# Score and maxima matmuls over 64 rows instead of 50 and 48, with zero rows behind

## The chip, the cores and the metric

One core of a Trainium2 chip runs the kernel. The time is device microseconds of one execution; the median of the runs is compared. TensorE is called PE in the profile (PEld is its loading of weights), VectorE DVE, ScalarE ACT, GpSimd POOL and SyncE, which issues most DMAs, SP.

## The reference

```python
x = A_x                                              # 1 x 2048 x 512
g = sigmoid((x * gate_w).sum(-1, keepdims=True))
a = dft_seq_re @ (x @ dft_hid_re.T) - dft_seq_im @ (x @ dft_hid_im.T)
q, k, v = split(x @ wqkv)                            # 32 heads of 16
b = concat(softmax(q @ k.T / 4) @ v) @ wo            # full attention, 2048 x 2048 per head
out = g * a + (1 - g) * b
```

All is float32.

## The kernel before

The sequence is 2048 long (16 tiles of 128, NT), the width 512 (4 tiles, KT). Products that need accuracy are done with numbers split into a high and a low part (`hi_lo`, L100), so that each takes three matmuls.

The stages, in order of time: q and k for all heads are computed and their high and low parts stored to DRAM (`evac_qk`, L200, through seven `hl` buffers on chip); then V (first eight tiles over all 128 rows, L397, then pairs of tiles on the two halves of the array, L365), its tiles emptied from PSUM by a copy on ScalarE and one on VectorE (`v_done`, L338 and L339); then x times the imaginary hidden DFT (L365 too). From there on the attention runs beside the other products of the reference.

Attention works on pairs of heads (16 pairs). For one pair `load_stacks` (L263) brings q and k from DRAM into `qs` and `ks`, tiles of 128 partitions by 2048, of which there are two each, used by turns. Each head has one half of the partitions, 64 rows from row 0 or 64: the first 48 hold three times 16 rows of high and low parts, so that one matmul over 48 rows gives the three products q_hi k_hi + q_hi k_lo + q_lo k_hi. The *maxima* matmul (`a_tile`, L278, matmul in L284) uses these 48 rows; VectorE reduces each result of 128 x 512 to the row's maxima (L286). When half of a pair's rows is done, `m_parts` and `m_rows` (L293 to L310) turn the negated maxima, high and low, into rows and write them by DMA into rows 48 and 49 of `qs` (L309, on SP or GpSimd). Rows 48 and 49 of `ks` hold ones; they are written once for each of the two tiles, by eight DMAs at the start (L322 to L325). The *score* matmul (`scores`, L761, matmul in L774) runs over 50 rows, and so yields scores with the maximum taken off; ScalarE takes their exponential (L775), and `pv` (L788, matmuls in L796) multiplies by V.

The order of the work on TensorE is written out by hand. In each segment (`segment`, L907) one half of the array does products of the DFT (64 rows, L451) while the other half does scores ("s") and maxima ("a"), and then both do `pv` ("|"). The digits name PSUM banks; scores and maxima use six:

```python
FULL = "s2 a3 s4 a1 s5 s2 a0 s3 a4 s1 a5 s2 a0 s3 a4 a1 | |"
```

FULL segments fill the long middle stage. Maxima run ahead of scores by LEAD = 44 steps of 64 per pair; the first 44 are done during the V and DFT products (`phase`, L358). V tiles use the three banks of `psS`. A plan by units (32 per pair) says when other work is issued; `load_stacks(p)` for p from 1 comes at unit 32 (p - 1) (L854, L855). SP issues its DMAs, and VectorE, ScalarE and GpSimd take their instructions, in the order in which the program writes them.

The tiles `vt`, `qs` and `ks` lie where the buffers of the q/k stage were. The lines around L317 set up what attention needs: ones on GpSimd, the ones of `vt`, `load_stacks(0)`, four loads of `wo`, the eight DMAs into `ks`.

Of the kernel before, what the change touches and what calls it, by code (L numbers as in the profile page):

```python
# [9 lines left out]
F32 = mybir.dt.float32  # L10
# [6 lines left out]
S = 2048  # L17
# [14 lines left out]
def mix_kernel(ctx: ExitStack, tc: tile.TileContext, xa_t, xa, wqkv, w_hid, w_seq, wo, gate_w, out):  # L32
# [5 lines left out]
    nc = tc.nc  # L38
# [31 lines left out]
    dram = ctx.enter_context(tc.tile_pool(name="dram", bufs=1, space=DRAM))  # L70
# [7 lines left out]
    yr_d = [dram.tile([P, D], F32, name=f"yr{t}") for t in range(NT)]  # L78
    yg_d = [dram.tile([P, D], F32, name=f"yg{t}") for t in range(NT)]

    wo_d = [dram.tile([P, 2, D], F32, name=f"wo{kt}") for kt in range(KT)]
    oh_d = [[dram.tile([P, 2, S // 2], F32, name=f"oh{hf}{ct}") for ct in range(3)] for hf in range(2)]
    r_d = [[dram.tile([2, 4, S // 2], F32, name=f"r{hf}{ct}") for ct in range(4)] for hf in range(2)]
# [4 lines left out]
    z = const.tile([P, NT], F32, name="z")  # L88
# [31 lines left out]
    def staged(src):  # L120
        raw = st1.tile([P, D], F32, name="raw", bufs=RAW)
        i = nc.sync.dma_start(raw, src)
        if behind:
            tc.add_manual_dep(i.ins, behind.pop().ins.name,
                              mybir.DependencyInfo(mybir.DependencyClass.Sync, mybir.DependencyReason.DATA))
        return raw
# [64 lines left out]
    with tc.tile_pool(name="qk", bufs=1, reuse_waits="tile") as pool:  # L191
# [38 lines left out]
        for tb in range(4):  # L230
# [4 lines left out]
            for c in range(2):  # L235
                if tb == 0 and c == 0:
                    pss = [bank() for _ in range(4)]
                    for kt in range(KT):
                        x = xab[tb][:, :, :, kt * P:(kt + 1) * P]
# [20 lines left out]
    qs = [main.tile([P, S], F32R, name=f"qs{i}", tag=f"qs{i}") for i in range(2)]  # L260
    ks = [main.tile([P, S], F32R, name=f"ks{i}", tag=f"ks{i}") for i in range(2)]

    def load_stacks(p):  # L263
        q_t, k_t = qs[p % 2], ks[p % 2]
        for h in range(2):
            rows = slice((2 * p + h) * DH, (2 * p + h + 1) * DH)
            o = 64 * h

            for i, (qv, kv) in enumerate(((0, 0), (0, 1), (1, 0))):
                part = slice(o + 16 * i, o + 16 * i + 16)  # L270
                nc.sync.dma_start(q_t[part].bitcast(F32), qk_d[0][qv, rows])
                nc.sync.dma_start(k_t[part].bitcast(F32), qk_d[1][kv, rows])


    deferred = []
# [2 lines left out]
    def a_tile(i, h, ps=None, bank=None):  # L278
        p, j = divmod(i, 64)
        qt, kb = divmod(j, 4)  # L280
        if ps is None:
            ps = psA.tile([P, 512], F32, "a", bank)
        r = slice(64 * h, 64 * h + 48)
        nc.tensor.matmul(ps, qs[p % 2][r, qt * P:(qt + 1) * P], ks[p % 2][r, kb * 512:(kb + 1) * 512],  # L284
                         start=True, stop=True)
        user = nc.vector.tensor_reduce(mx[p % 2][:, h, qt, kb:kb + 1], ps, AX.X, ALU.max)  # L286
        hf = j // 32
        a_left[p, hf] = a_left.get((p, hf), 64) - 1
        if not a_left[p, hf]:
            deferred.extend((partial(m_parts, p, hf), partial(m_rows, p, hf)))  # L290
        return user
# [22 lines left out]
            deferred.pop(0)()  # L314


    ones = st1.tile([2, 2 * D], F32, name="hl", bufs=4)  # L317
    nc.gpsimd.memset(ones, 1.0)
    nc.gpsimd.memset(vt[:, :, :, 16:17], 1.0)
    load_stacks(0)  # L320
    wos = [staged(wo[:, kt]) for kt in range(KT)]
    for i in range(2):  # L322
        for h in range(2):
# [34 lines left out]
    def phase(pair, half, maxima):  # L358
        nonlocal a_next, user
        before, user = user, None  # L360
        for j in range(12):
            for x, (ps, ops, done) in enumerate(pair):
                st, mv = ops[j]
                r = slice(64 * (half ^ x), 64 * (half ^ x) + 64)
                i = nc.tensor.matmul(ps, st[r], mv[r], start=not half and not j, stop=half == 1 and j == 11)  # L365
                if not j and not x and half:
                    tc.add_manual_dep(i.ins, before.ins.name,
                                      mybir.DependencyInfo(mybir.DependencyClass.Sync, mybir.DependencyReason.DATA))
            if maxima and j in (3, 9):
                for h in range(2):  # L370
                    used = a_tile(a_next, h, acc if h and j == 9 else None)
                user = user or used
                a_next += 1
        if half:
            for ps, ops, done in pair:
                done(ps)
        if deferred:
            deferred.pop(0)()
# [382 lines left out]
    def scores(u, qb, h, bank=(psS, "s"), number=None):  # L761
        p, r = divmod(u, 32)
        hf, kt = divmod(r, 16)
        q0 = hf * 1024 + qb * 512
        if u >= UNITS - 16:

            blk, kt = divmod(kt, 8)
            q0, kt = 1024 + blk * 512, 2 * kt + qb
        if u not in pts:
            pts[u] = work.tile([P, 4, 512], F32, name="pt", bufs=4)  # L770
        pool, name = bank
        ps = pool.tile([P, 512], F32, name=name) if number is None else pool.tile([P, 512], F32, name, number)
        rr = slice(64 * h, 64 * h + 50)
        nc.tensor.matmul(ps, ks[p % 2][rr, kt * P:(kt + 1) * P], qs[p % 2][rr, q0:q0 + 512], start=True, stop=True)  # L774
        return nc.scalar.activation(pts[u][:, 2 * qb + h], ps, AF.Exp, bias=0.0, scale=DH ** -0.5)  # L775

# [77 lines left out]
    for p in range(1, NP):  # L854
        at(32 * (p - 1), load_stacks, p)  # L855
# [37 lines left out]
    def score(kind, h, number=None):  # L893
        nonlocal exponential
        x = next(streams[h][kind == "a"], None)
        if x:
            users.append((kind, a_tile(*x, bank=number) if kind == "a" else scores(*x, number=number)))
            if kind == "s":
                exponential = users[-1][1]
# [84 lines left out]
    for bank in (*three[:1], *three):  # L984
        scores(*next(streams[1][0]), bank)
# [8 lines left out]
    for u in range(valued + 2, UNITS, 2):  # L994
        run_plan(u)
        for i in range(4):
            if i == 2:
                for gen, n in whole[u]:
                    pump(gen, n)
                if u == 506:  # L1000
                    last_pairs[0].turn()
                elif u == 508:
                    last_pairs[0].back()
            for h in range(2):
                scores(u + i // 2, i % 2, h, three[h])
        values()
        values()
# [40 lines left out]
```

## Time and profile before

| what | value |
|---|---|
| median of 3 runs | 1698.75 us (1698.6 to 1699.33) |
| span of the profiled execution | 1696.8 us |
| PE busy | 1689.2 us |
| DVE busy | 1366.7 us |
| ACT busy | 1138.6 us |
| POOL busy | 449.6 us |
| mean granted TensorE clock | 0.999 |

The span goes from the first to the last instruction of one profiled execution; the time of a run holds a little more than that. Rows of groups read: line, engine, operation, what it writes and from what, shapes, count | busy time, mean ns of one | idle time of the engine before them and what ended it. Rows in order of time read: start in us, duration in us, engine, line, operation, count and, in brackets, idle time before. "SPq" is the queue of SyncE. Names drop buffer numbers: `hl` is a pair of high and low parts, `acc` the result of `pv`, `pt` the exponentials, `mx` the maxima, `d` a PSUM bank of the DFT products.

### The profile page before, as it was taken

The page shows a single profiled execution, that of the slowest core. Times are in us where ns is not written, and L with a number is a line of the kernel's source. Part 1 is how long each engine was busy: PE and PEld are TensorE (multiplying, and loading weights), DVE is VectorE, ACT ScalarE, POOL GpSimd, SP SyncE. Part 2 cuts the span into 40 slices and gives each one's busy share as a digit, 9 for nine tenths or more (in the row PEclk, how much of TensorE's full clock was granted, in tenths as well). Part 3 has the DMA queues.
Part 4 walks back from the last instruction along what each step waited for, and adds up shares of the span by engine and source line. Part 5 has one row for each costly group of instructions (what it writes and reads, how often), then busy time and mean ns, then how long its engine had stood idle before and what let it go on. Part 6 is the DMA issues. An engine that isn't in the chain of part 4 may idle for free.

```text
span 1696.8 us, 33721 instructions
## 1 busy us (share of the span) xinstructions
PE 1689.2 (100%) x13040; PEld 1076.1 (63%) x13040; DVE 1366.7 (81%) x2313; ACT 1138.6 (67%) x2242; POOL 449.6 (26%) x554
## 2 busy tenths in 40 slices
PE   9999999999999999999999999999999999999998
PEld 7888855556666666666666666666666666655544
DVE  5439888888888888888888888888888888889854
ACT  5212377777766777666777677776667776678886
POOL 0101122322222333222222343322323343211110
PEclk9999999999999999999999999999999999999999
DMA  8963600314141434314156435224141535362114
GB/s 294 344 146 132 161 8 13 47 39 76 57 76 46 88 98 97 73 39 82 38 95 243 96 108 109 68 63 77 50 83 58 120 111 101 129 187 39 36 30 138
DMA packets 82274, 165.10 MB, mean 97 GB/s; under 512 B 19460, under 2 KB 19954, under 8 KB 78274
## 3 DMA queue, kind: packets, MB, share of 16 engines
q1 hardware_dynamic: 77874, 161.99, 37.1%
q8 instruction: 103, 1.69, 0.4%
q0 software_dynamic: 3808, 0.30, 0.2%
q10 hardware_dynamic: 432, 0.66, 0.1%
q14 instruction: 57, 0.47, 0.1%
HBM read 107.73 MB, written 54.52 MB: 96 GB/s over the span
## 4 chain that ended last, share of the span: by engine, by line
PE 99%; DMA 0%; DVE 0%; DVEq 0%; ACT 0%; SPq 0%; issue 0%
PE d L451 33%; PE acc L796 27%; PE s L774 14%; PE a L284 12%; PE s L365 3%; PE s L397 1%; PE d L365 1%; PE acc L782 1%; PE a L106 1%; PE s L107 1%; PE a L107 1%; PE s L106 1%; PE s L105 1%; PE a L105 1%; PE s L451 1%; PE a L451 0%
## 5 line engine op out<-in xcount | busy, mean ns | idle before, releaser
L286 DVE TENSOR_REDUCE mx<-a 128x1 f32<-128x512 f32 x2026 | 1239.9, 681 | 213.1 <-PE a L284 199.1
L775 ACT ACTIVATE pt<-s 128x512 f32<-128x512 f32 x2006 | 1023.2, 620 | 403.0 <-PE s L774 390.5
L774 PE MATMUL s<-qs,ks 50*128 50x512 f32 x2006 | 794.0, 422 | 0.0
L284 PE MATMUL a<-ks,qs 48*128 48x512 f32 x2026 | 744.5, 398 | 0.0
L451 PE MATMUL d<-xab,ch 64*128 64x512 f32 x2016 | 647.8, 396 | 0.0
L774 PEld LDWEIGHTS s<-qs,ks 50*128 50x128 f32 x2006 | 365.4, 185 | 228.5 <-issue 177.5
L796 PE MATMUL acc<-pt,vt 128*17 128x512 f32 x3968 | 484.2, 596 | 0.0
L284 PEld LDWEIGHTS a<-ks,qs 48*128 48x128 f32 x2026 | 370.3, 186 | 53.2 <-DVE mx L286 23.2
L451 PE MATMUL d<-xab,cl 64*128 64x512 f32 x1008 | 399.4, 396 | 0.0
L451 PEld LDWEIGHTS d<-xab,ch 64*128 64x128 f32 x2016 | 366.7, 184 | 21.6
L435 POOL CAST ch<-craw 128x512 fp32r<-128x512 f32 x126 | 77.1, 612 | 549.1 <-PE a L284 282.2
L796 PEld LDWEIGHTS acc<-pt,vt 128*17 128x17 f32 x3968 | 102.3, 96 | 184.7 <-issue 184.5
L451 PEld LDWEIGHTS d<-xab,cl 64*128 64x128 f32 x1008 | 185.7, 184 | 10.5
L436 POOL TENSOR_TENSOR cl<-craw,ch 128x512 fp32r<-128x512 f32 x126 | 162.1, 1287 | 10.2
L309 POOL DMA_DIRECT2D qs<-mt x119 | 67.0, 568 | 150.3 <-DVE mt L303 147.8
L451 PE MATMUL d<-wre,xab 64*128 64x512 f32 x336 | 90.5, 402 | 0.0
L451 PEld LDWEIGHTS d<-wre,xab 64*128 64x128 f32 x336 | 59.0, 185 | 38.4 <-issue 23.3
L451 PE MATMUL d<-wo_hl,o_hl 64*128 64x512 f32 (+1 forms) x246 | 68.1, 409 | 0.0
L451 PEld LDWEIGHTS d<-wo_hl,o_hl 64*128 64x128 f32 (+1 forms) x246 | 42.3, 185 | 29.5 <-issue 12.1
L101 ACT CAST hl<-s 128x512 fp32r<-128x512 f32 x28 | 16.1, 587 | 58.5 <-PE s L365 31.4
L647 POOL TENSOR_TENSOR yp<-yp,few 128x512 f32<-128x512 f32 x12 | 15.4, 1283 | 112.4 <-ACT few L646 112.4
L469 POOL CAST xab<-y 128x512 fp32r<-128x512 f32 x16 | 9.8, 611 | 127.8 <-ACT y L467 99.6
(168 smaller groups left out, 1009.6 us busy)
## 6 DMA issues: line engine op xcount, KB each, us to landing
craw<-w_seq SPq DMA_DIRECT2D x128, 256.0 KB
qk<-hl SPq DMA_DIRECT2D x32, 512.0 KB
qs<-qk SPq DMA_DIRECT2D x96, 128.0 KB
ks<-qk SPq DMA_DIRECT2D x96, 128.0 KB
b<-hl SPq DMA_DIRECT2D x16, 512.0 KB
xab<-b SPq DMA_DIRECT2D x16, 512.0 KB
o<-oe SPq DMA_DIRECT2D x62, 128.0 KB
oh<-nh SPq DMA_DIRECT2D x12, 512.0 KB
```

What stands on the lines that cost most here:

```text
L105: nc.tensor.matmul(ps, sh, mh, start=first, stop=False)
L106: nc.tensor.matmul(ps, sh, ml, start=False, stop=False)
L284: nc.tensor.matmul(ps, qs[p % 2][r, qt * P:(qt + 1) * P], ks[p % 2][r, kb * 512:(kb + 1) * 512], start=True, stop=True)
L286: user = nc.vector.tensor_reduce(mx[p % 2][:, h, qt, kb:kb + 1], ps, AX.X, ALU.max)
L309: (nc.gpsimd if own else nc.sync).dma_start(rows.rearrange("v (q b c) -> v b q c", q=8, b=4)[:, b], mt[hf][32 * b + h:32 * b + 32:2])
L365: i = nc.tensor.matmul(ps, st[r], mv[r], start=not half and not j, stop=half == 1 and j == 11)
L435: nc.gpsimd.tensor_copy(h1, raw)
L436: nc.gpsimd.tensor_tensor(l1, raw, h1.bitcast(F32), ALU.subtract)
L451: i = nc.tensor.matmul(self.ps, st[r], mv[r], start=not self.begun, stop=stop)
L774: nc.tensor.matmul(ps, ks[p % 2][rr, kt * P:(kt + 1) * P], qs[p % 2][rr, q0:q0 + 512], start=True, stop=True)
L775: return nc.scalar.activation(pts[u][:, 2 * qb + h], ps, AF.Exp, bias=0.0, scale=DH ** -0.5)
L796: i = nc.tensor.matmul(acc[32 * j:32 * j + 17], vt[:, kt, p, 16 * h:16 * h + 17], pt[:, j], start=kt == 0, stop=kt == NT - 1)
```

## The change

The matmuls of scores and maxima take all 64 rows of their half. For that the rows behind the values must be zero: rows 32 to 63 of each half of all four tiles are set to zero at the start, `qs` by GpSimd and `ks` by VectorE, ahead of the first load (the loads then fill rows 32 to 47, the maxima and ones rows 48 and 49). Since `qs` still holds the maxima of two pairs ago in rows 48 and 49 when a pair's maxima are computed, each load from the third pair on writes zeros there, from a piece of DRAM that is filled once. The block that loads the first pair moves ahead of the ones. Numbers of lines after it shift by up to 9.

```diff
+    z_d = dram.tile([2, S], F32, name="z")
...
                 nc.sync.dma_start(k_t[part].bitcast(F32), qk_d[1][kv, rows])
+            if p > 1:
+                nc.sync.dma_start(q_t[o + 48:o + 50].bitcast(F32), z_d)
...
-        r = slice(64 * h, 64 * h + 48)
+        r = slice(64 * h, 64 * h + 64)
         nc.tensor.matmul(ps, qs[p % 2][r, qt * P:(qt + 1) * P], ks[p % 2][r, kb * 512:(kb + 1) * 512],
...
+    for i in range(2):
+        for h in range(2):
+            for x, eng in ((qs, nc.gpsimd), (ks, nc.vector)):
+                eng.memset(x[i][64 * h + 32:64 * h + 64].bitcast(F32), 0.0)
+        if not i:
+            load_stacks(0)
+            nc.sync.dma_start(z_d, qs[0][48:50].bitcast(F32))
     ones = st1.tile([2, 2 * D], F32, name="hl", bufs=4)
     nc.gpsimd.memset(ones, 1.0)
     nc.gpsimd.memset(vt[:, :, :, 16:17], 1.0)
-    load_stacks(0)
...
-        rr = slice(64 * h, 64 * h + 50)
+        rr = slice(64 * h, 64 * h + 64)
         nc.tensor.matmul(ps, ks[p % 2][rr, kt * P:(kt + 1) * P], qs[p % 2][rr, q0:q0 + 512], start=True, stop=True)
```

## The prediction

> **What bounds the kernel now.** I read the page first (busy times, chain, groups), then the order of time in one segment of the long middle stage, then the stretch from 92 to 105 us, where the change puts its new instructions.
>
> ```profile
> span 1696.8 us, 33721 instructions
> PE 1689.2 (100%) x13040; PEld 1076.1 (63%) x13040; DVE 1366.7 (81%) x2313; ACT 1138.6 (67%) x2242; POOL 449.6 (26%) x554
> PE 99%; DMA 0%; DVE 0%; DVEq 0%; ACT 0%; SPq 0%; issue 0%
> L774 PE MATMUL s<-qs,ks 50*128 50x512 f32 x2006 | 794.0, 422 | 0.0
> L284 PE MATMUL a<-ks,qs 48*128 48x512 f32 x2026 | 744.5, 398 | 0.0
> L451 PE MATMUL d<-xab,ch 64*128 64x512 f32 x2016 | 647.8, 396 | 0.0
> L774 PEld LDWEIGHTS s<-qs,ks 50*128 50x128 f32 x2006 | 365.4, 185 | 228.5 <-issue 177.5
> L284 PEld LDWEIGHTS a<-ks,qs 48*128 48x128 f32 x2026 | 370.3, 186 | 53.2 <-DVE mx L286 23.2
> L451 PEld LDWEIGHTS d<-xab,ch 64*128 64x128 f32 x2016 | 366.7, 184 | 21.6
> ```
>
> TensorE holds 99% of the chain, so whatever makes it wait is added to the end. The six groups hold the main question: do rows cost anything? Weight loads of 48, 50 and 64 rows take 186, 185 and 184 ns. Matmuls of 48 and 64 rows take 398 and 396; the 422 of the 50-row ones is a mean with waits in it. So 64 rows should take what 48 take. The order of the changed program shows the matmuls of TensorE one for one as before; there is none to save.
>
> One segment of the middle stage runs from 704.52 to 710.43:
>
> ```profile
> 704.52 0.49 PE L774 MATMUL s<-qs,ks 50*128 50x512 f32 x1
> ...
> 707.84 0.39 PE L451 MATMUL d<-xab,ch 64*128 64x512 f32 x1
> 708.01 0.39 PE L284 MATMUL a<-ks,qs 48*128 48x512 f32 x1
> 708.07 0.39 PE L451 MATMUL d<-xab,cl 64*128 64x512 f32 x1
> 708.24 0.42 PE L284 MATMUL a<-ks,qs 48*128 48x512 f32 x1
> 708.59 0.63 PE L796 MATMUL acc<-pt,vt 128*17 128x512 f32 x4
> ```
> ```profile
> 708.16 0.18 PEld L284 LDWEIGHTS a<-ks,qs 48*128 48x128 f32 x1
> ```
> ```profile
> 705.05 4.04 ACT L775 ACTIVATE pt<-s 128x512 f32<-128x512 f32 x8 [1.87 <-PE s L774]
> ```
> ```profile
> 710.43 0.50 PE L774 MATMUL s<-qs,ks 50*128 50x512 f32 x1
> ```
>
> The half of the array with scores and maxima starts its last matmul at 708.24, the other half at 708.07; the first one ends the segment. What holds it is ScalarE: eight exponentials in 4.04 us, (4.04 - 0.62) / 7 = 0.49 apart (0.62 is the mean of L775 on the page). The sixth ends at about 705.05 + 5 x 0.49 + 0.62 = 708.12; it reads bank 1, into which the last maxima matmul writes (pattern FULL: s1, then a1), and that matmul's weight load starts at 708.16, not at 708.01 with the matmul before it. So even if rows did cost a few ns, ScalarE would hide nearly all of the gain.
>
> **The change part by part.**
>
> (1) 50 and 48 rows become 64. Taken as 0. Bounds: the chain of exponentials starts 0.53 us after the segment, behind two or three score matmuls. If each came 5 ns earlier, a segment would gain about 13 ns; the stage holds some 192 segments of 5.91 us, so at most 2.5 us. Downwards, the last weight load waits 0.15 us for its bank, so 5 ns more on each matmul would also hide, except for the same 2.5 us.
>
> (2) For each pair from the third on, SP issues two DMAs that write zeros into rows 48 and 49 (28 in all).
>
> ```profile
> 482.36 0.52 SPq L271 DMA_DIRECT2D qs<-qk  x1
> ...
> 489.10 0.30 SPq L272 DMA_DIRECT2D ks<-qk  x1
> 490.21 5.22 SPq L425 DMA_DIRECT2D craw<-w_seq  x2
> ```
>
> They lengthen a load of twelve by 2 x 0.42 us, on SP. The code issues it at the first unit of pair p - 1; that pair's maxima lead by 44 of 64 steps, two to a unit, so the next pair's first maxima come 10 units later, about 10 x 2.95 = 29 us (two units per segment). The load takes 7 us. The DFT loads behind it move by about 1 us. Cost 0 while that slack lasts; with 1 us of waiting per pair it would be 14.
>
> (3) Eight memsets of 32x2048 and a DMA of zeros to DRAM, ahead of the first pair's loads. Four (qs) are on GpSimd, four (ks) on VectorE. This is the part that I expect to see.
>
> ```profile
> 95.22 0.08 DVE L226 DVE_READ_ACCUMULATOR raw<-raw,gwb 128x1 f32 x1
> 96.52 0.42 DVE L339 COPY vt<-s 128x256 f32<-128x256 f32 x1 [1.21 <-ACT vt L338]
> 99.24 0.42 DVE L339 COPY vt<-s 128x256 f32<-128x256 f32 x1 [2.30 <-ACT vt L338]
> ```
> ```profile
> 93.19 17.16 PE L397 MATMUL s<-wv,xab 128*128 128x512 f32 x75
> ```
> ```profile
> 95.26 0.33 SPq L271 DMA_DIRECT2D qs<-qk  x1
> 98.86 0.31 SPq L272 DMA_DIRECT2D ks<-qk  x1
> ```
> ```profile
> SPq L272 <- DMA qk<-hl: 3.2, 1, 3.2
> ```
>
> ks lies where the q/k stage had its buffers, the last of which are still being stored. Before, SP waited for those stores, 3.2 us until 98.86, and nothing else did. In the changed program the first ks memset waits for the same stores, and it stands in VectorE's queue ahead of the copies that empty the V tiles (96.52, then every 2.72 us). So VectorE stands still to 98.86 and then does four memsets before the first copy. The V tiles turn in three banks: the fourth, due at 93.19 + 3 x 2.72 = 101.35, needs the first copy. TensorE waits there.
>
> Price of a memset of 2048 elements:
>
> ```profile
> L410 DVE MEMSET acc<- 128x512 f32 x1 | 0.5, 485 | 0.1
> L172 DVE MEMSET xab<- 128x128 f32 x1 | 0.2, 165 | 0.8 <-PEq L1041 0.8
> L611 DVE TENSOR_TENSOR o_l<-o_raw,o_l 128x1024 fp32r<-128x1024 f32 x1 | 1.2, 1224 | 0.0
> L611 DVE TENSOR_TENSOR o_lnh<-o_raw,o_lnh 128x512 fp32r<-128x512 f32 x1 | 0.7, 692 | 0.0
> L610 DVE CAST o_l<-o_raw 128x1024 fp32r<-128x1024 f32 x1 | 0.7, 694 | 2.3 <-POOL o_raw L624 2.3
> L610 DVE CAST o_lnh<-o_raw 128x512 fp32r<-128x512 f32 x1 | 0.4, 420 | 0.0
> ```
>
> The memset's own rows give (485 - 165) / 384 = 0.83 ns per element, so 485 + 1536 x 0.83 = 1765 ns. At the pace of the tensor_tensor it would be 1224 + 2 x 532 = 2288, at that of the cast 694 + 2 x 274 = 1242. I take the own rows, though one writes PSUM and the other SBUF. Then: 98.86 + 4 x 1.77 = 105.94; the first copy, 0.42, ends at 106.36; 0.1 for TensorE to take it up (a weight load, as at 708.16 and 708.24): 106.45. The wait is 106.45 - 101.35 = **5.1 us**, with 3.0 and 7.2 as its ends.
>
> [...]
>
> A pause of 5 us also has a price after it:
>
> ```profile
> 1690.25 0.39 PE L731 MATMUL a<-w,o 32*128 32x512 f32 x2
> ```
> ```profile
> 1690.00:1697.00 7.00, 0.64 (x12) 0.19 (x4) 2.60 (x4) 0.69 (x1) 1.26 (x1) 0.86 0.49 187
> ```
> ```profile
> 1.06 4.21 PE L177 MATMUL d<-xab 128*128 128x512 f32 x9 [1.06 <-DVE xab L172]
> 5.11 0.62 PE L242 MATMUL s<-xab,wh 128*128 128x512 f32 x1
> ```
>
> At the end TensorE falls idle at 1690.64, and the granted clock of the last 7 us is 0.86: at half clock that is 0.14 x 7 / 0.5 = 2.0 us, so the drop came at about 1695.0, 4.4 us into the pause. At the start nine matmuls took 4.05 us, 0.45 each, where 0.227 is usual (2.72 / 12): 2.0 us lost until the clock was up. The new pause lasts from about 101.5 to 106.45, 4.95 us, over 4.4. I add **2.0 us**, with 0 as its other end.
>
> [...]
>
> GpSimd's four memsets are beside the path: its queue is idle from 94.0 to 113.9, and what waits for it (qs loads, the ones for ks) is needed at the first maxima only, near 119, which move back with TensorE. The z store is 16 KB on SP there.
>
> **The sum.** 0 + 0 + 5.1 + 2.0 = 7.1 us. TensorE is never idle from there to 1640, so nothing takes it up again. The span of the profiled execution, 1696.8, becomes 1703.9; the median of the runs shown, 1698.75, stands 1.95 above that span, so I expect 1698.75 + 7.1 = 1705.9 us.
>
> **The rivals.**
> A. *The memsets are quick.* At the cast's pace, 1.24 us each, VectorE is free at 103.8, TensorE goes on at 104.35, the wait is 3.0 us and the pause too short for the clock: 1701.8, not slower by what can be told. The point that decides is a memset of 1.33 us, for a wait of 3.4. For it: VectorE has a row at that pace. Against: both memset rows.
> B. *The clock holds.* Only the wait: 1703.9. For it: a pause just 0.55 us over the one that was seen to suffice.
> C. *Rows do cost something.* The exponentials start 13 ns earlier in 192 segments, -2.5, and the V and FNet stages, which have 44 pairs of maxima, gain perhaps 1: 1702.3 with the wait. For it: the maxima and score groups have longer means than the DFT's. Against: equal weight loads, and ScalarE's chain. A real gain of over 0.2% would need more than 50 ns per segment, which that chain doesn't leave.
> D. *The added loads make pairs wait*, 1 us for each of 14: 1720. Against: 29 us of slack.
>
> **How the numbers follow.** Forecast 0.53, with the memset anywhere from 1.6 to 2.3 us (1704 to 1709); B 0.20; A 0.10; C 0.12; D 0.05. The range 1701.0 to 1709.0 holds the forecast with both ends of its memset, B, and most of A and C; D and A with C together are left out. A measurement can tell about 0.2% here, 3.4 us. Slower: the forecast, B, D and a part of C, 0.80. Within: most of A, a part of C, 0.16. Faster: 0.04, what is left of C with A.
>
> **What would show it.** Of the profile after: one gap on TensorE between about 101.5 and 106.5, with its releaser the V copy on VectorE; four memset rows on VectorE behind 98.86, each near 1.77; matmuls at 0.45 us apart behind the gap, with a lower granted clock there; a segment of the middle stage still 5.91 us long, and weight loads of 64 rows at 184 to 186 ns. The prediction is wrong if the gap is absent or far shorter, if segments change by more than 15 ns, or if the first maxima of a pair wait for DMA.

## The result, and the profile after

The changed kernel takes 1707.99 us (median of 4 runs, 1707.9 to 1708.65) against 1698.84 for the kernel before in the same session (4 runs, 1698.6 to 1699.33): 9.15 us longer, a ratio of 1.0056 with a 95% interval from 1.0043 to 1.0068. The forecast was 1705.9, that is 7.1 us longer.

From the page of the changed kernel, the lines that answer to those of before: span, busy times, chain, and the groups of TensorE.

```profile
span 1705.9 us, 33851 instructions
PE 1691.7 (99%) x13040; PEld 1066.3 (63%) x13040; DVE 1374.4 (81%) x2317; ACT 1138.6 (67%) x2242; POOL 456.9 (27%) x558
PE 99%; DVE 1%; DMA 0%; issue 0%; DVEq 0%; ACT 0%
L783 PE MATMUL s<-qs,ks 64*128 64x512 f32 x2006 | 795.9, 423 | 0.0
L287 PE MATMUL a<-ks,qs 64*128 64x512 f32 x2026 | 742.1, 397 | 0.0
L460 PE MATMUL d<-xab,ch 64*128 64x512 f32 x2016 | 647.9, 396 | 0.0
L783 PEld LDWEIGHTS s<-qs,ks 64*128 64x128 f32 x2006 | 363.6, 184 | 235.8 <-issue 178.4
L287 PEld LDWEIGHTS a<-ks,qs 64*128 64x128 f32 x2026 | 368.6, 185 | 60.3 <-DVE mx L289 23.1
```

The span grew by 9.1 us, as the time did. TensorE's instructions are as many as before, their durations within 1 ns, and a share of 1% on the chain has gone to VectorE: some waiting on VectorE is new. It lies in one place. From the order of time, first TensorE, then VectorE, around the V tiles (brackets: idle time before):

```profile
93.18 8.32 PE L406 MATMUL s<-wv,xab 128*128 128x512 f32 x36
108.46 3.78 PE L406 MATMUL s<-wv,xab 128*128 128x512 f32 x8 [6.96 <-DVE vt L348]
```
```profile
99.45 1.76 DVE L323 MEMSET ks<- 32x2048 f32 x1 [4.15 <-DMA qk<-hl]
101.69 1.76 DVE L323 MEMSET ks<- 32x2048 f32 x1 [0.48 <-issue]
103.94 1.76 DVE L323 MEMSET ks<- 32x2048 f32 x1 [0.48 <-issue]
106.18 1.76 DVE L323 MEMSET ks<- 32x2048 f32 x1 [0.48 <-issue]
107.98 1.09 DVE L348 COPY vt<-s 128x256 f32<-128x256 f32 x3
```

Three V tiles (36 matmuls) go through; the fourth, due at 93.18 + 3 x 2.72 = 101.34, starts at 108.46, when the first copy has emptied a bank. The copy stands behind the four memsets, and the first memset behind the stores of q and k. The wait is 7.1 us.

Behind the gap eight matmuls take 3.78 us, where eight usually take 7 x 0.227 + 0.39 = 1.98. The windows of the same kernel give the granted clock (second number from behind the commas: start:end, us, busy time of PE, PEld, DVE, ACT and POOL with counts, PEclk, DMA share, GB/s):

```profile
101.00:105.80 4.80, 0.50 (x3) 0.07 (x1) 3.74 (x3) 0.38 (x1) 2.98 (x3) 1.00 1.13 137
105.80:112.70 6.90, 4.24 (x10) 3.38 (x11) 2.85 (x4) 0.00 (x0) 0.00 (x0) 0.51 0.96 138
112.70:120.00 7.30, 7.30 (x33) 6.01 (x33) 1.28 (x3) 1.14 (x3) 0.00 (x0) 1.00 0.28 99
```

PEclk is the third number from the end: full up to 105.8, half up to 112.7, full again. The records of the clock put the half at 105.89 to 112.71, 6.8 us. TensorE works in the last 4.25 us of it, from 108.46 on, and loses half of that, 2.1 us. So 7.1 + 2.1 = 9.2 us, and the whole difference is accounted for.

GpSimd's memsets lie beside that, as expected (first line here); so do the zero rows that each later pair loads (the second, from SP's queue, in the same load as the lines of 482 to 489 us shown of before):

```profile
98.91 3.64 POOL L323 MEMSET qs<- 32x2048 f32 x2 [4.86 <-issue]
```
```profile
493.84 0.28 SPq L275 DMA_DIRECT2D qs<-z  x1
```

A segment of the middle stage, TensorE and then ScalarE, the answer to the one at 704.52:

```profile
713.30 0.49 PE L783 MATMUL s<-qs,ks 64*128 64x512 f32 x1
...
716.85 0.39 PE L460 MATMUL d<-xab,cl 64*128 64x512 f32 x1
717.02 0.41 PE L287 MATMUL a<-ks,qs 64*128 64x512 f32 x1
717.37 1.91 PE L805 MATMUL acc<-pt,vt 128*17 128x512 f32 x16
719.21 0.49 PE L783 MATMUL s<-qs,ks 64*128 64x512 f32 x1
```
```profile
716.93 0.18 PEld L287 LDWEIGHTS a<-ks,qs 64*128 64x128 f32 x1
```
```profile
713.83 4.04 ACT L784 ACTIVATE pt<-s 128x512 f32<-128x512 f32 x8 [1.87 <-PE s L783]
```

It is 719.21 - 713.30 = 5.91 us long, its last maxima matmul starts 3.72 us after its first, as before (708.24 - 704.52), and the exponentials start 0.53 us after it and last 4.04 us, as before. The weight load of the last maxima matmul (the line of PEld) starts 0.05 us behind the end of the sixth exponential; in the kernel before it does so in every one of the 192 segments of this pattern. Worked out from the traces over these 192, the mean length is 5.905 us before and 5.908 after.

### The profile page after: what moved, and what is told of

Read it like the earlier page. It is cut to its first block, busy times and chain, and to the rows that moved or that the text cites. A ratio compares the mean times of both kernels' runs of the same rounds, so it can differ in the third digit from the quotient of the medians.

```text
span 1705.9 us, 33851 instructions
## 1 busy us (share of the span) xinstructions
PE 1691.7 (99%) x13040; PEld 1066.3 (63%) x13040; DVE 1374.4 (81%) x2317; ACT 1138.6 (67%) x2242; POOL 456.9 (27%) x558
## 4 chain that ended last, share of the span: by engine, by line
PE 99%; DVE 1%; DMA 0%; issue 0%; DVEq 0%; ACT 0%
PE acc L805 27%; PE d L460 27%; PE s L783 18%; PE a L287 14%; PE s L374 3%; PE s L406 1%; PE acc L791 1%; PE d L374 1%; PE a L108 1%; PE s L106 1%; PE a L106 1%; PE s L108 1%; PE s L107 1%; PE a L107 1%; PE s L460 1%; PE a L460 0%
## 5 line engine op out<-in xcount | busy, mean ns | idle before, releaser
L783 PE MATMUL s<-qs,ks 64*128 64x512 f32 x2006 | 795.9, 423 | 0.0
L287 PE MATMUL a<-ks,qs 64*128 64x512 f32 x2026 | 742.1, 397 | 0.0
L783 PEld LDWEIGHTS s<-qs,ks 64*128 64x128 f32 x2006 | 363.6, 184 | 235.8 <-issue 178.4
L287 PEld LDWEIGHTS a<-ks,qs 64*128 64x128 f32 x2026 | 368.6, 185 | 60.3 <-DVE mx L289 23.1
L445 POOL TENSOR_TENSOR cl<-craw,ch 128x512 fp32r<-128x512 f32 x126 | 162.1, 1287 | 10.2
L102 ACT CAST hl<-s 128x512 fp32r<-128x512 f32 x28 | 16.1, 587 | 58.1 <-PE d L374 17.4
```

Source lines behind the costliest of these rows:

```text
L445: nc.gpsimd.tensor_tensor(l1, raw, h1.bitcast(F32), ALU.subtract)
```

## The experiments

The first four runs take the change apart, the next seven ask what rows cost and what hides it, the last looks at a memset by itself. The kernel before ran beside them: 1698.63 us (27 runs) beside the first four, 1698.49 (7) beside the next three, 1698.51 (18) beside the four after them and 1698.80 (7) beside the last.

### All zeros on GpSimd

```diff
+    def zero(i):
+        for h in range(2):
+            for x in (qs, ks):
+                nc.gpsimd.memset(x[i][64 * h + 32:64 * h + 64].bitcast(F32), 0.0)
+    zero(0)
+    load_stacks(0)
...
     nc.gpsimd.memset(vt[:, :, :, 16:17], 1.0)
+    zero(1)
```

> All eight memsets on GpSimd, the second tiles' behind the ones; 64 rows and the zero loads as in the changed kernel. If the 9.2 us are VectorE's memsets ahead of the V copies and the clock behind the pause, TensorE has no gap near 101 us and the time is about 1698.7 us: that of before, less some 0.6 in the V and FNet stages, where the matmuls behind a maxima pair are no longer late, and more some 0.5 in the segments beside the zero loads. Rival: if 64 rows or the zero loads cost time in the middle stage, it stays over 1702.

Measured: 1698.51 us (11 runs), ratio 0.9999 (0.9990 to 1.0008). TensorE and GpSimd in order of time:

```profile
93.32 19.88 PE L408 MATMUL s<-wv,xab 128*128 128x512 f32 x87
```
```profile
90.57 1.80 POOL L323 MEMSET qs<- 32x2048 f32 x1 [37.69 <-DMA qk<-hl]
99.26 1.80 POOL L323 MEMSET ks<- 32x2048 f32 x1 [6.88 <-DMA qk<-hl]
```

The V matmuls run through in one piece of 87. The same memset waits for the same stores, on a queue that empties no V tile, and costs nothing. So all of the 9.15 us is the place of four memsets; 64 rows, GpSimd's memsets and the 28 zero loads together cost and bring nothing that can be measured.

### The same, with 50 and 48 rows

The kernel above, with the matmuls back at their old rows and everything else of the change in place:

```diff
-        r = slice(64 * h, 64 * h + 64)
+        r = slice(64 * h, 64 * h + 48)
...
-        rr = slice(64 * h, 64 * h + 64)
+        rr = slice(64 * h, 64 * h + 50)
```

> As e1_gpsimd_zero, with the matmuls back at 48 and 50 rows (the memsets, the zero loads and the moved block stay). If rows are worth only the V and FNet stages, it is about 0.5 us above e1, 1699.3 us, and a segment of the middle stage is 5.905 us in both. Rival: if the rows matter in the middle stage, the two differ by 12 us (15 matmuls by 4 ns by 192 segments).

Measured: 1698.65 us (11 runs), ratio 1.0000 (0.9991 to 1.0009), 0.14 us over the kernel with 64 rows. That is within the noise: in the full kernel the rows are worth nothing that a measurement can tell.

### Two memsets on VectorE in place of four

```diff
+    for h in range(2):
+        for x, eng in ((qs, nc.gpsimd), (ks, nc.vector)):
+            eng.memset(x[0][64 * h + 32:64 * h + 64].bitcast(F32), 0.0)
+    load_stacks(0)
...
     nc.gpsimd.memset(vt[:, :, :, 16:17], 1.0)
+    for h in range(2):
+        for x in (qs, ks):
+            nc.gpsimd.memset(x[1][64 * h + 32:64 * h + 64].bitcast(F32), 0.0)
```

> Only the first ks tile's two memsets stay on VectorE ahead of the V copies, the other two go to GpSimd; 64 rows. If the price is 2.24 us for each memset in front of the copies, TensorE's gap shrinks from 7.0 to about 2.5 us, too short for the clock to drop, and the time is 1708.0 - 4.5 - 2.1 = 1701.4 us. Rival: if the wait for the last q/k stores (to 99 us) is the price and not the memsets, the gap stays near 7 us and the time near 1708.

Measured: 1701.76 us (10 runs, 1701.06 to 1703.17), ratio 1.0020 (1.0011 to 1.0029). Order of time on VectorE and TensorE, then the clock in windows:

```profile
99.68 1.76 DVE L322 MEMSET ks<- 32x2048 f32 x1 [4.14 <-DMA qk<-hl]
101.93 1.76 DVE L322 MEMSET ks<- 32x2048 f32 x1 [0.48 <-issue]
```
```profile
104.20 9.06 PE L407 MATMUL s<-wv,xab 128*128 128x512 f32 x32 [2.47 <-DVE vt L349]
```
```profile
102.00:104.00 2.00, 0.00 (x0) 0.00 (x0) 1.97 (x2) 0.15 (x1) 1.95 (x2) 1.00 1.05 123
104.00:107.50 3.50, 3.30 (x8) 2.62 (x9) 0.81 (x3) 0.00 (x0) 2.39 (x2) 0.51 0.98 112
```

The wait came out as expected: the fourth V tile, due at 93.42 + 3 x 2.72 = 101.58, starts 2.6 us late, 4.5 us less than with four memsets. So two memsets fewer in front of the copies take 4.5 us off the wait, two of the distances of 2.24 us from start to start. The clock did not come out: it was taken to hold through so short a pause, and in the profiled execution it fell, 2.4 us into a pause of 2.5, for 3.4 us, which costs 1.65. The ten times fall into two groups, six from 1701.06 to 1701.78 and four from 1702.83 to 1703.17, 1.6 us apart; the profiled one is of the second. By their times, then, a pause of 2.5 us can cost the clock or not, from one execution to the next; only the one execution has a trace.

### Four memsets, but TensorE kept busy in the pause

Thirty matmuls more into a bank that nobody reads, between the third and the fourth V tile:

```diff
+            if s == 3:
+                spin = psD.tile([P, 512], F32, name="d")
+                for i in range(30):
+                    nc.tensor.matmul(spin, *ops[i % 12], start=True, stop=True)
```

> The changed kernel with 30 more matmuls into a PSUM bank that nobody reads, ahead of the fourth V tile: they take 30 x 0.227 = 6.8 us of the pause. If the halved clock behind the pause costs 2.1 us, the time is 1705.9 us and the granted clock is full throughout. Rival: if the clock costs nothing of its own, the time stays at 1708.0.

Measured: 1705.91 us (4 runs, 1705.64 to 1706.12), ratio 1.0043 (1.0027 to 1.0058). TensorE in order of time, and a window:

```profile
101.51 6.96 PE L408 MATMUL d<-wv,xab 128*128 128x512 f32 x30
108.68 4.60 PE L410 MATMUL s<-wv,xab 128*128 128x512 f32 x19 [0.21 <-DVE vt L348]
```
```profile
108.00:112.00 4.00, 3.79 (x18) 2.79 (x17) 1.26 (x4) 0.27 (x1) 0.00 (x0) 1.00 0.98 112
```

The V tile starts as late as in the changed kernel, but the clock stays full and 19 matmuls take 4.60 us. 1707.99 - 1705.91 = 2.1 us is the price of the clock, 1705.91 - 1698.63 = 7.3 that of the wait (7.1 by the trace).

### Half the work for ScalarE and VectorE, with either number of rows

To see what rows cost when nothing hides it, exponentials and maxima take only the first 256 of 512 columns, so half of both is left out; `pv` reads the 256 columns twice and keeps its length. One kernel has 48 and 50 rows, the other 64, zeros on GpSimd in both.

```diff
-        user = nc.vector.tensor_reduce(mx[p % 2][:, h, qt, kb:kb + 1], ps, AX.X, ALU.max)
+        user = nc.vector.tensor_reduce(mx[p % 2][:, h, qt, kb:kb + 1], ps[:, :256], AX.X, ALU.max)
...
-        return nc.scalar.activation(pts[u][:, 2 * qb + h], ps, AF.Exp, bias=0.0, scale=DH ** -0.5)
+        return nc.scalar.activation(pts[u][:, 2 * qb + h, :256], ps[:, :256], AF.Exp, bias=0.0, scale=DH ** -0.5)
...
```

> As e2_gpsimd_zero_48_50, but each exponential and each maximum takes only the first 256 of 512 columns (half of the exponentials and maxima is left out; pv reads the half twice, so TensorE's work stays). ScalarE and VectorE no longer hold any bank. If rows cost about 4 ns per matmul on TensorE, which they hid before, the score half of a segment now runs at 235 ns per matmul to the end and a segment is near 5.81 us.

> As e5_half_work_48_50 with 64 rows. If rows cost 4 ns per matmul, hidden by the waits for ScalarE and VectorE in the full kernel, it is now 15 x 4 ns = 60 ns per segment faster than e5, some 12 us in all. Rival: if rows cost nothing in the middle stage, the two agree within 1 us.

Measured: 1667.08 us with 48 and 50 rows, 1648.75 with 64 (4 runs each; ratios to the kernel before 0.9815, from 0.9801 to 0.9830, and 0.9707, from 0.9691 to 0.9723). The groups of scores and maxima on the two pages, 48 and 50 rows first:

```profile
L785 PE MATMUL s<-qs,ks 50*128 50x512 f32 x2006 | 767.4, 409 | 0.0
L287 PE MATMUL a<-ks,qs 48*128 48x512 f32 x2026 | 738.1, 395 | 0.0
```
```profile
L785 PE MATMUL s<-qs,ks 64*128 64x512 f32 x2006 | 760.7, 406 | 0.0
L287 PE MATMUL a<-ks,qs 64*128 64x512 f32 x2026 | 726.8, 390 | 0.0
```

The rows do cost time: 18.3 us, half as much again as the 12 expected. Durations show little of it (3 and 5 ns); the distance between starts does. By the trace, the 16 scores and maxima of a segment take 3618 ns from first start to last with 48 and 50 rows and 3537 with 64: 81 / 15 = 5.4 ns for each. The DFT's half of the array, whose matmuls are the same in both, goes from 3550 to 3538. A segment falls from 5.783 to 5.699 us; 192 x 0.084 = 16.1 us, and the rest lies in the stages before and after.

### 56 rows

The kernel with all zeros on GpSimd, and both slices at 56 rows: does the price shrink with the rows that are missing?

> As e1_gpsimd_zero with 56 rows for scores and maxima (six or eight of them zero). Look at the V stage: behind a pair of 48-row maxima the next four matmuls start 232, 238, 233 and 230 ns apart, 25 ns more than four times 227; with 64 rows all are at 227. If the delay goes with the rows that are missing, 56 rows show about half, 12 ns; if it is that the rows fall short of the half at all, 25 ns; if it came of 48 alone, none.

One run: 1698.99 us. In this part of the V stage a pair of maxima matmuls, one on each half of the array, stands behind every six pairs of V matmuls, and TensorE doesn't wait there; so the distance from pair to pair is its own. Each block shows one pair and the second pair behind it, of before, of 56 rows and of the changed kernel (where the profile lists the other matmul of the pair in a row of its own):

```profile
131.73 0.40 PE L284 MATMUL a<-ks,qs 48*128 48x512 f32 x2
134.95 0.40 PE L284 MATMUL a<-ks,qs 48*128 48x512 f32 x2
```
```profile
131.64 0.40 PE L287 MATMUL a<-ks,qs 56*128 56x512 f32 x2
134.87 0.40 PE L287 MATMUL a<-ks,qs 56*128 56x512 f32 x2
```
```profile
132.83 0.39 PE L287 MATMUL a<-ks,qs 64*128 64x512 f32 x1
136.00 0.39 PE L287 MATMUL a<-ks,qs 64*128 64x512 f32 x1
```

3.22 and 3.23 us against 3.17. To three digits the trace has a pair every 1.613 us with 48 rows, every 1.613 with 56, and every 1.587 with 64, over 13 pairs. So 26 ns a pair are lost with 8 rows missing, and no more with 16.

### Which engine hides it: half of the exponentials, or half of the maxima

The two edits above, one at a time, with either number of rows.

> Zeros all on GpSimd, 50 and 48 rows, and exponentials over the first 256 of 512 columns only (pv reads them twice); the maxima stay whole. It leaves out half of the exponentials. Question: which engine hid the price of rows, ScalarE (theory S, as the prediction says) or VectorE's reductions (rival V)? By S a segment is free of its hold once the exponentials are short: 1667 us, as with both halved. By V nothing changes: 1698.6. If both hold: in between, nearer 1698.

> As the run before with 64 rows in scores and maxima (half of the exponentials left out, maxima whole). By S 1649 us, that is 18 us below the run before. By V 1698.5, difference 0. If both hold, the difference is a few us.

> Zeros all on GpSimd, 50 and 48 rows, exponentials whole, and maxima over the first 256 of 512 columns only; half of the maxima's work is left out. By S nothing changes: 1698.6 us. By V 1667. If both hold: in between.

> As the run before with 64 rows (half of the maxima's work left out, exponentials whole). By S 1698.5 us, difference to the run before 0. By V 1649, difference 18.

Measured, with the mean length of the 192 segments worked out from the traces. The ratios to before are 0.9913 (0.9896 to 0.9931 and 0.9898 to 0.9929) with half of the exponentials, 0.9994 (0.9984 to 1.0004) and 0.9985 (0.9975 to 0.9994) with half of the maxima:

| exponentials | maxima | 48 and 50 rows | 64 rows | segment, us |
|---|---|---|---|---|
| whole | whole | 1698.65 | 1698.51 | 5.905, 5.907 |
| whole | half | 1697.39 | 1695.88 | 5.908, 5.909 |
| half | whole | 1683.94 | 1683.92 | 5.847, 5.852 |
| half | half | 1667.08 | 1648.75 | 5.783, 5.699 |

Neither theory was right by itself: ScalarE holds first, VectorE right behind it. With the exponentials halved the time falls by 14.6 us, not by 31, and rows still make no difference; a segment is then 5.85 us long, and halving the maxima too shortens it further, so VectorE sets that length. With the maxima alone halved nothing changes in the segments (1697.39 can't be told from before; the 1.5 us to 1695.88 lie outside them). Only with both out of the way does the number of rows set the length. So to be worth 18 us, 64 rows need the length that ScalarE sets for a segment to fall by 5.905 - 5.699 = 0.21 us, and the one that VectorE sets by 5.85 - 5.70 = 0.15, an estimate from this table.

The trace of the kernel before shows both holds at work. Of the 16 weight loads for scores and maxima in a segment, four (the 6th, 12th, 14th and 16th) start 0.05 us behind the end of an exponential, and three (the 8th, 10th and 15th) 0.05 to 0.06 us behind the end of a reduction, by the median over 192 segments. With 64 rows and all zeros on GpSimd, the sixth matmul starts 16 ns sooner (1.268 us after the first instead of 1.284); at the thirteenth nothing of it is left (3.002 and 2.999).

### The order of the four memsets

The changed kernel's memsets start 2.24 us apart, with rows of 1.76; from the first memset to the first copy it is 107.98 - 99.45 = 8.53 us, 2.13 for each of the four. Is the row too short, or is something held between them? The same four in another order: partitions 32, 32, 96, 96, instead of 32, 96, 32, 96.

```diff
+    for h in range(2):
+        for i in range(2):
+            nc.vector.memset(ks[i][64 * h + 32:64 * h + 64].bitcast(F32), 0.0)
     for i in range(2):
         for h in range(2):
-            for x, eng in ((qs, nc.gpsimd), (ks, nc.vector)):
-                eng.memset(x[i][64 * h + 32:64 * h + 64].bitcast(F32), 0.0)
+            nc.gpsimd.memset(qs[i][64 * h + 32:64 * h + 64].bitcast(F32), 0.0)
```

> The changed kernel with the same four ks memsets on VectorE in another order: both tiles' rows 32 to 63 first, then both tiles' rows 96 to 127, so that the first two start at the same partition, and the last two. In the changed kernel, where the start partition changes at each, they start 2.24 us apart with rows of 1.76 and 0.48 idle between. Theory A: a memset takes about 2.13 us whatever the order (its row is too short); starts stay 2.1 to 2.25 apart everywhere and the time 1708.0. [...]

Measured: 1708.12 us (4 runs, 1706.38 to 1709.11), ratio 1.0056 (1.0039 to 1.0072), too wide to tell a difference of a microsecond; the rows of VectorE tell more:

```profile
99.01 1.76 DVE L322 MEMSET ks<- 32x2048 f32 x1 [4.12 <-DMA qk<-hl]
101.15 1.76 DVE L322 MEMSET ks<- 32x2048 f32 x1 [0.38 <-issue]
103.38 1.76 DVE L322 MEMSET ks<- 32x2048 f32 x1 [0.47 <-issue]
105.52 1.76 DVE L322 MEMSET ks<- 32x2048 f32 x1 [0.38 <-issue]
107.31 1.09 DVE L350 COPY vt<-s 128x256 f32<-128x256 f32 x3
```

The starts are 2.14, 2.23 and 2.14 us apart. All three lie between 2.1 and 2.25, as theory A expected: two memsets that start at the same partition are 2.14 us apart, 0.38 more than the row, and where the start partition changes, 0.1 more. What the 0.38 is made of isn't shown. The copy starts 1.79 us behind the last memset, 0.03 us behind the end of its row; so the missing time lies between two memsets, and either belongs to the second one, ahead of its row, or is a pause. TensorE resumed 0.26 us earlier after its first V matmul than in the changed kernel (107.79 - 92.77 = 15.02 against 108.46 - 93.18 = 15.28), and lost more than that to the clock, which was at half from 103.37 to 113.61:

```profile
107.79 5.49 PE L408 MATMUL s<-wv,xab 128*128 128x512 f32 x12 [6.70 <-DVE vt L350]
```
```profile
109.00:113.00 4.00, 4.00 (x11) 3.12 (x10) 0.00 (x0) 0.00 (x0) 0.00 (x0) 0.50 0.92 180
```

## Why the prediction was right, and where it was off

The place, the two terms and the order of events were right. The time came out 2.1 us over the forecast, and all of that lies in one term, the wait behind the memsets.

**Rows, taken as 0: right in its sum, wrong in one reason.** The segment stayed at 5.91 us and the rows brought nothing that can be measured, because ScalarE's exponentials hold the banks of scores and maxima matmuls. That cover is shown, and a second one behind it, VectorE's reductions, which the prediction did not have. Wrong was "So 64 rows should take what 48 take", from equal durations: they take 5.4 ns less each where nothing else holds, close to the 5 ns that the prediction had tried as a bound. Rival C therefore had a true mechanism with hardly any room: the pairs in the V stage come 26 ns sooner, and with all zeros on GpSimd the time from the first V matmul to the first score matmul is 195.10 - 93.32 = 101.78 us with 64 rows, 195.31 - 92.93 = 102.38 with 50 and 48. Those 0.6 us stand in place of the "perhaps 1" of rival C, and its 2.5 us in the segments did not come.

**The zero loads, 0: right.** With them in place, two kernels tie with the one before.

**The memsets on VectorE: right place, right wait, price too low.** The step that was off is "I take the own rows", 1765 ns. The row came out at 1.76 us as worked out, but the next memset starts only 2.24 us after the last one. From the first memset to the first copy it took 107.98 - 99.45 = 8.53 us (three distances of 2.24 and one of 1.80, ahead of the copy), against 4 x 1.77 = 7.08: 1.45 us more. The first one began at 99.45, not at 98.86 with SP, 0.59 more. Together 2.0, and the wait was 7.1, just inside the ends of 3.0 and 7.2. Why the first began later than SP's DMA is open: in the trace the semaphore instructions of its line stand at 98.84 and 98.91, so its waits ended when SP's did. The runs show 2.14 from start to start for memsets at one partition, 2.23 to 2.25 where the start partition changes, and 1.79 to 1.80 to a copy. The slope between two rows says how rows grow with length; it says nothing of the time between one row and the next. The prediction's range was also looser than its sum: a memset of 1.6 to 2.3 us gives 1705.2 to 1708.0 by it, not 1704 to 1709, and the measured 1708.0 is the upper end of that.

**The clock, 2.0: right, and shown by itself** as 2.1 us; the size is partly luck. The clock fell 4.4 us into the pause (105.89 - 101.50), as long as at the end of the kernel before (1695.03 - 1690.64). The five falls compared below came 2.3 to 4.4 us after the last matmul, so the forecast pause of 4.95 us would by these have lost the clock too. What a fall costs depends on how much of the half-speed stretch TensorE works through: 2.1 us here, 1.65 with two memsets, (113.61 - 107.79) / 2 = 2.9 with the other order. The prediction's second witness, the nine matmuls at the start, shows a pace of half speed only: the records of the clock begin at 5.43 us, so no granted clock stands beside it.

**Rivals.** A, quick memsets, needed 1.33 us: out. B, a clock that holds: out for this pause, by its times true in six of ten runs for the shorter one. D, pairs waiting for loads: out.

## What to carry to other kernels

Put work that only prepares a later stage on a queue through which nothing on the critical path drains: the same four memsets cost 9 us on VectorE and nothing on GpSimd. Price an instruction by the distance from its start to the next start on its engine, not by its row alone, and look at what comes next: a memset here took 2.14 to 2.25 us ahead of another one and 1.79 ahead of a copy, with a row of 1.76; matmuls of fewer rows cost 5 ns that the durations don't show. Before a saving on TensorE is counted, shorten the engines that hold its banks in an experiment: here two stood one behind the other.

## What the runs showed of the hardware

The clock's half-speed stretches were 3.4, 6.8 and 10.2 us long (two memsets, the changed kernel, the other order), that is one, two and three times 3.41. The clock fell after 2.4 us of the pause with two memsets (104.09 - 101.74), after 2.3 with the other order (103.37 - 101.09) and after 4.4 in the changed kernel; at the ends of the kernel before and of the changed one it fell 4.4 and 3.6 us (1703.32 - 1699.74) after the last matmul. In the 3.41 us ahead of each of these five falls TensorE's matmuls took at most 1.1 us (1.1 in the runs with two memsets and with the other order, none in the three other cases), and in the 3.41 us ahead of those at least 2.4. The clock was full again 3.3 us after TensorE's first matmul behind the pause with two memsets (107.50 - 104.20), 4.25 after it in the changed kernel (112.71 - 108.46) and 5.8 with the other order (113.61 - 107.79). What makes it fall and rise isn't shown.

In the V stage, each pair of matmuls over 48 or 56 of the 64 rows of a half took 26 ns more of TensorE's time than a pair over all 64 (1.613 against 1.587 us from one maxima pair to the next). In the segments, with ScalarE and VectorE out of the way, scores and maxima over 50 and 48 rows start 5.4 ns further apart, and the DFT products on the other half of the array take longer from the first to the last start too (3550 against 3538 ns). What in TensorE does this was not tried.
